# Seven products for all six chunks of a first matmul, in two passes, with two input sums on GpSimd and a group's output assembled in the next group

## The chip, the cores and the metric

The kernel runs on one core of a Trainium2 chip. The metric is the device time of one execution in microseconds (us); less is better. Five engines work side by side, each with its own queue of instructions in program order: TensorE (PE in the profile, with its weight loads as PEld), VectorE (DVE), ScalarE (ACT), GpSimd (POOL) and SyncE (SP), which here only issues DMAs. An instruction waits at the head of its queue until what it needs is there, and everything behind it waits with it.

## The reference, cut to what matters

```python
# x: (8, 4224, 192) float32; weight: (8 heads, 7 taps)
w = softmax(weight, axis=-1)
y[b, s, d] = sum_k w[d // 24, k] * x_pad[b, s + k, d]     # 6 rows of zeros in front of x
xn = (y - mean(y)) / sqrt(var(y) + 1e-6) * g_ln            # over d
out = y + relu(xn @ w_ch1) @ w_ch2                         # 192 -> 768 -> 192
```

Everything is float32. The mean and `g_ln` are folded into the first weight, and 1/sqrt(var) is applied to the result of the second matmul, since relu lets a positive factor through.

## The kernel before, in words

**Tiling.** The rows are cut into 18 groups. Groups 0 to 2 are small and set up the work; groups 3 to 17 have 128 partitions x 16 rows of 192 each, and the change is about those. A group g passes through two matmuls: `up_mixed(g)` (192 to 768, with relu) and `down_fast(g)` (768 to 192). While TensorE works on group g, VectorE finishes the convolution of group g+1 and ScalarE starts that of g+2.

**Seven products.** Both matmuls are done by a scheme that multiplies 2 x 2 blocks with seven products instead of eight, at the price of sums of blocks before and after. A block product has four results c11, c12, c21 and c22; two of the seven products are added into a result that stays in PSUM, others are brought to SBUF (`evict`, a ScalarE copy of the four banks) and added there. `close(c, banks, part)` adds a product to a result already in SBUF: ScalarE copies the banks to a spare tile, and GpSimd issues a DMA that adds that tile to the result (L582). In the last group VectorE adds straight from PSUM instead (L614). In the first matmul the 768 columns are six chunks of 128. Four go through the seven products (2 of each 3, `PAIR`), each product 48 matmul instructions of 256 columns (L521); the two left over are computed plainly (`plain`, 48 matmul instructions of 512 columns each). Products alternate between two sets of four PSUM banks, so a product needs the eviction of the product before the last one. In the second matmul each product is 72 instructions of 256 columns in three steps c (L762), with a ScalarE copy of one bank after each step (L768).

The products of `down_fast` are called d1 to d7 here, in their order: d1 `a[0,0]*b[0]`, d2 `a[1,0]*w2sums[2]`, d3 `a[1,1]*w2sums[3]`, d4 `a[0,1]*b[2]` (no copy, VectorE adds it, L801), d5 `a[1,1]*w2sums[1]`, d6 `a[0,0]*w2sums[0]`, d7 `a[0,1]*b[3]`. d2 needs `lower_sum` (L736); d5, d6 and d7 need the first, second and third triple of the nine `half_sum` instructions (L727) on VectorE. d6 accumulates on the banks of d5 and d7 on those of d6, so each step of d7 needs the copy of the same step of d6.

**Order on the engines around the change.** VectorE, from the start of an `up_mixed(g)`: the output of group g-1 (`finish_fast`: three transposes, an addition, three transposes, L822 and L824), eight tap instructions of the convolution of g+1 (`conv`, L408; each tap is eight instructions, one a head), the last sum of y (L578), 28 taps, `lower_sum`, four taps, then in `down_fast(g)` the transpose of y (L419), ten row statistics (`moments`, L439), `half_sum`, the three additions of d4, six statistics and three sums of y (L574 to L576).

ScalarE: the evictions and closings of the first matmul, with scalings of the output rows of g-1 between them (`scale`, L849, one row each); relus of c11 and c22; then the copies of d1 to d7, between which the first two taps of group g+2 are put (`first_tap` L383 and `second_tap` L394, 16 instructions). The second tap is written to a spare tile `tb` and added to y by two DMAs (L397).

GpSimd issues the adding DMAs: the closings, the taps of `tb`, and `add_to_out` (L856), which adds the scaled output rows to `out` in two halves, rows 0 to 8 and 8 to 16, both within `up_mixed(g)` or just behind it. It also works out 1/sqrt(var) for two groups at a time (`root`, L457 to L470). SP stores y (L477) and loads x.

**Tiles with one buffer.** Each of the pools behind `tb`, `cs`, `ot`, `ys` and `yt` has one buffer. A new tile of such a pool can be written only when all readers of the old one are through, a DMA included. `tb` is in turn the second tap's tile and a room for closings (`parts`). `ot`, the output of a group, is written by the transposes of `finish_fast` and read by the two DMAs of `add_to_out`.

Of the kernel before, what the change touches and what calls it, by code (L numbers as in the profile page):

```python
# [16 lines left out]
def kernel(  # L17
# [34 lines left out]
    P = 128  # L52
# [223 lines left out]
    w1sums = consts.tile([P, 4, CH, PAIR * P], F32, name="w1sums")  # L276
# [236 lines left out]
    def rows_of_tiles(banks, left, right, first=True, last=True):  # L513
# [3 lines left out]
        for c in range(left.shape[2]):  # L517
            for i in range(chunks):
                for q in range(NQ):
                    rows = slice(C * q, C * q + C)  # L520
                    nc.tensor.matmul(  # L521
                        banks[:, q, i * w : i * w + w], right[rows, c, P * i : P * i + P],
                        left[rows, :, c, :], start=(first and c == 0 and i == 0),
                        stop=(last and c == left.shape[2] - 1), skip_group_check=chunks > 1,
                    )
# [22 lines left out]
    def quarters_of_w1():  # L548
        return [
            w1[:, CH * k : CH * k + CH, P * f : P * (f + PAIR)] for k in range(2) for f in (0, FC)  # L550
        ]

    def sums_of_quarters(dst, b11, b12, b21, b22):

        for v, a, b in ((0, b12, b11), (1, b22, 0), (2, b12, b22), (3, b21, 1)):
            a, b = (dst[:, u] if isinstance(u, int) else u for u in (a, b))
            nc.vector.tensor_tensor(dst[:, v], a, b, op=ALU.subtract)
# [10 lines left out]
    def sums_of_y(g):  # L568
# [3 lines left out]
        ysums[g] = s1, s2, s3 = [room[:, v] for v in range(3)]  # L572
        a11, a12, a21, a22 = quarters_of_y(g)
        nc.vector.tensor_tensor(s1, a21, a22, op=ALU.add)  # L574
        nc.vector.tensor_tensor(s2, s1, a11, op=ALU.subtract)
        nc.vector.tensor_tensor(s3, a21, a11, op=ALU.subtract)  # L576
        yield
        nc.vector.tensor_tensor(s2, a12, s2, op=ALU.subtract)  # L578
# [5 lines left out]
    def up_mixed(g, last_sum):  # L584
# [4 lines left out]
        assert groups[g][2] == 2 * HJ and PAIR * W == 512  # L589
# [3 lines left out]
        b11, b12, b21, b22 = quarters_of_w1()  # L593
        s1, s2, s3 = ysums[g]
        (c11, c12), (c21, c22) = [
            [a[:, h, e, 0:PAIR].rearrange("p f q j t -> p f q (j t)") for e in range(2)]
            for h in range(2)
        ]
# [5 lines left out]

        def evict(banks, dst, relu=False, i=slice(0, PAIR)):
            src = banks.rearrange("p q (f w) -> p f q w", w=W)[:, i]
            nc.scalar.activation(dst, src, AF.Relu) if relu else nc.scalar.copy(dst, src)  # L607

        def close(c, banks, part, i=slice(0, PAIR)):


            if last:
                src = banks.rearrange("p q (f w) -> p f q w", w=W)[:, i]
                nc.vector.tensor_tensor(c[:, i], c[:, i], src, op=ALU.add)  # L614
                return
            evict(banks, part, i=i)
            whole = "p f q w -> p (f q w)"
            add_by_dma(c[:, i].rearrange(whole), part.rearrange(whole))

        def plain(f, banks):  # L620
            rows_of_tiles(banks, yt[g][:, 0 : 2 * HJ], w1[:, :, f * P : f * P + P])
            evict_up(g, f, banks)


        chain, other = take_set(), take_set()
        turn[0] += 4
        done = groups[g - 1][2]
        rooms = parts(bpool, "tb"), parts(cpool, "cs")
        first, second = (r[:, 0:PAIR] for r in rooms)
# [8 lines left out]

        rows_of_tiles(chain, a11, b11, True, False)
        evict(chain, c11)  # L640
        rows_of_tiles(other, a12, b21)
        close(c11, other, first)
        rows_of_tiles(chain, s2, w1sums[:, 1], False, False)
        evict(chain, c21)
        act_scales(0, 1)
        taps_of_next(2, 3)
        next(last_sum)
# [8 lines left out]
        rows_of_tiles(other, s3, w1sums[:, 2], True, False)  # L656
        evict(other, c22)
        act_scales(1, 2)
        rows_of_tiles(chain, s1, w1sums[:, 0], False, False)
        close(c22, chain, second)  # L660
        act_scales(2, 3)
        rows_of_tiles(other, a22, w1sums[:, 3], False)
        for i, room in enumerate(rooms):
            close(c21, other, room[:, PAIR : PAIR + 1], slice(i, i + 1))
        act_scales(3, 4)
        rows_of_tiles(chain, s2, b22, False)
        evict(chain, c12, True)
        nc.scalar.activation(c11, c11, AF.Relu)
        act_scales(4, 7)
        taps_of_next(3, 6)  # L670
        taps_of_next(6, K, heads=(0, H // 2))
        plain(PAIR, other)
        nc.scalar.activation(c22, c22, AF.Relu)
        if not last:
            scale(g - 1, 7, 10)
            add_to_out(g - 1, 0, 8)
        lower_sum(g, (PAIR,))
        lower_sum(g, range(PAIR))
        taps_of_next(6, K, heads=(H // 2, H))
        plain(PAIR + FC, chain)  # L680
        if last:

            rest = a[:, 1, 0, 0:PAIR, :, fast[g] :]
            for f in range(PAIR):
                nc.scalar.activation(rest[:, f], rest[:, f], AF.Relu)
        else:
            scale(g - 1, 10, done)
            add_to_out(g - 1, 8, done)
# [54 lines left out]
    def down_fast(g):  # L743
# [254 lines left out]
```

## Time and profile before

| what | us |
| --- | --- |
| median of 3 runs | 969.36 (969.23 to 969.53) |
| span of the profiled execution, first to last instruction | 967.8 |
| TensorE busy in it | 956.1 |
| VectorE busy | 870.7 |
| ScalarE busy | 640.2 |
| one group in the middle (541.76 to 597.73) | 55.97 |
| of it the second matmul, then the first of the next group | 27.33 and 28.64 |

The time of the profiled execution as a whole is not listed apart from its span; the median of the runs is 1.56 us above that span. A line of the timeline gives the start in us from the span's start, the time it took, the engine, the line of the kernel, the operation, output and input, the count of instructions merged into it, and in brackets idle time just before it with what ended it. L12 is line 12 of the kernel.

### The profile page before, as it was taken

How to read it: one execution, taken by the hardware profiler on the slowest of the kernel's cores; microseconds unless marked ns; L12 is line 12 of the kernel's file. 1: busy time of each engine (PE TensorE's matmuls, PEld its weight loads, DVE VectorE, ACT ScalarE, POOL GpSimd, SP SyncE). 2: the span in 40 equal slices, each digit the busy share in tenths (PEclk: the TensorE clock that was granted, in tenths of full speed). 3: DMA queues.
4: the chain of work that ended last, by engine and by line, in shares of the span. 5: the costliest groups of instructions: out<-in, count | busy, mean ns of one | idle time of the engine just before them, and what ended most of it. 6: DMA issues, size and time to landing. Idle time of an engine off the chain costs nothing.

```text
span 967.8 us, 36017 instructions
## 1 busy us (share of the span) xinstructions
PE 956.1 (99%) x16194; PEld 670.3 (69%) x16194; DVE 870.7 (90%) x1489; ACT 640.2 (66%) x1014; POOL 201.1 (21%) x355
## 2 busy tenths in 40 slices
PE   7999999999999999999999999999999999999997
PEld 6886585857668585766758576675857667685767
DVE  7999998898998979898998989899898989989837
ACT  5625677585957758595876858587685858675351
POOL 2005311411133111411114011321104111230400
PEclk9999999999999999999999999999999999999999
DMA  8243887697896869789686978969697886766221
GB/s 204 93 151 109 177 204 224 127 181 211 156 271 126 246 127 192 200 154 271 132 246 125 210 183 150 265 132 253 128 226 170 147 253 136 177 123 110 30 56 68
DMA packets 29960, 163.17 MB, mean 169 GB/s; under 512 B 3567, under 2 KB 9839, under 8 KB 22126
## 3 DMA queue, kind: packets, MB, share of 16 engines
q0 software_dynamic: 22704, 97.53, 53.4%
q1 hardware_dynamic: 6798, 63.34, 17.1%
q8 instruction: 127, 2.08, 0.8%
q14 instruction: 27, 0.22, 0.1%
q10 hardware_dynamic: 304, 0.00, 0.0%
HBM read 38.95 MB, written 50.33 MB: 92 GB/s over the span
## 4 chain that ended last, share of the span: by engine, by line
PE 98%; DMA 1%; DVE 0%; issue 0%; SPq 0%
PE ps L521 49%; PE ps L762 41%; PE ps L707 6%; DMA xg<-in_x_dram 1%; PE ps L320 1%; DMA ga<-in_moe_g_ln_dram 0%; PE ps L344 0%; PE ps L349 0%; DVE y L863 0%; PE ps L332 0%; DVE ot L888 0%; SPq L165 0%; DVE ot L873 0%; DVE y L876 0%
## 5 line engine op out<-in xcount | busy, mean ns | idle before, releaser
L408 DVE SCALAR_TENSOR_TENSOR y<-xg,taps,y 128x384 f32<-128x384 f32 (+3 forms) x734 | 368.1, 580 | 0.7 <-issue 0.5
L521 PE MATMUL ps<-yt,w 32*128 32x256 f32 (+3 forms) x3744 | 287.7, 459 | 0.0
L521 PEld LDWEIGHTS ps<-yt,w 32*128 32x128 f32 x3744 | 188.4, 185 | 90.7 <-issue 80.8
L762 PE MATMUL ps<-room,w2sums 128*32 128x256 f32 (+1 forms) x4320 | 233.8, 375 | 0.0
L762 PEld LDWEIGHTS ps<-room,w2sums 128*32 128x32 f32 x4320 | 140.8, 110 | 87.5
L762 PE MATMUL ps<-room,w 128*32 128x256 f32 (+1 forms) x3240 | 179.8, 375 | 0.0
L727 DVE TENSOR_TENSOR room<-room 128x1024 f32<-128x1024 f32 (+1 forms) x135 | 151.4, 1196 | 9.7 <-ACT part L768 9.7
L762 PEld LDWEIGHTS ps<-room,w 128*32 128x32 f32 x3240 | 104.0, 110 | 74.6 <-ACT ot L849 10.6
L768 ACT COPY cs<-ps 128x256 f32<-128x256 f32 (+1 forms) x180 | 62.9, 366 | 97.8 <-PE ps L762 97.1
L607 ACT COPY room<-ps 128x2048 f32<-128x2048 f32 x45 | 84.0, 1866 | 55.3 <-PE ps L521 53.9
L521 PE MATMUL ps<-ysums,w1sums 32*128 32x256 f32 x2160 | 119.4, 375 | 0.0
L521 PEld LDWEIGHTS ps<-ysums,w1sums 32*128 32x128 f32 x2160 | 110.9, 185 | 5.9 <-DVE room L614 0.3
L824 DVE STREAM_TRANSPOSE ot<-cs 128x512 f32<-128x512 f32 (+1 forms) x90 | 55.9, 672 | 56.8 <-DMA cs<-part 34.5
L511 ACT ACTIVATE room<-ps 128x2048 f32<-128x2048 f32 (+3 forms) x46 | 71.2, 1548 | 33.6 <-PE ps L521 33.6
L849 ACT ACTIVATE ot<-ot,r 128x192 f32<-128x192 f32 x232 | 90.9, 447 | 0.0
L383 ACT ACTIVATE y<-xg,taps 128x384 f32<-128x384 f32 (+3 forms) x141 | 73.3, 589 | 7.5 <-DMA out_dram<-y 6.9
L856 POOL DMA_DIRECT2D out_dram<-ot x40 | 34.2, 1086 | 198.4 <-ACT ot L849 137.1
L439 DVE BATCH_NORM_STATS2 st<-y 128x6 f32<-128x192 f32 x264 | 71.0, 343 | 0.0
L397 POOL DMA_DIRECT2D y<-tb x28 | 24.6, 1037 | 176.2 <-ACT cs L768 172.8
L736 DVE SCALAR_TENSOR_TENSOR room<-room 128x1024 f32<-128x1024 f32 (+1 forms) x45 | 51.5, 1199 | 8.6 <-ACT room L509 7.6
L394 ACT ACTIVATE tb<-xg,taps 128x384 f32<-128x384 f32 x112 | 58.1, 603 | 0.0
L419 DVE STREAM_TRANSPOSE yt<-y 128x3072 f32<-128x3072 f32 (+3 forms) x19 | 56.2, 2957 | 1.9
(104 smaller groups left out, 791.6 us busy)
## 6 DMA issues: line engine op xcount, KB each, us to landing
xg<-in_x_dram SPq DMA_DIRECT2D x15, 2112.0 KB, 15.2
out_dram<-ot POOLq DMA_DIRECT2D x29, 768.0 KB, 8.2
y<-tb POOLq DMA_DIRECT2D x28, 768.0 KB, 9.3
out_dram<-y SPq DMA_DIRECT2D x13, 1536.0 KB, 10.7
room<-parts_tb POOLq DMA_DIRECT2D x14, 1024.0 KB, 7.5
room<-parts_cs POOLq DMA_DIRECT2D x14, 1024.0 KB, 7.1
room<-parts_tb POOLq DMA_DIRECT2D x14, 512.0 KB, 9.3
room<-parts_cs POOLq DMA_DIRECT2D x14, 512.0 KB, 10.8
```

Of the source, the lines that this page charges most:

```text
L383: nc.scalar.mul(y[g][:, 0:n, cs], xg[g][:, 0:n, cs], taps[:, h, 0:1])
L394: nc.scalar.mul(tb[g][:, 0:n, cs], xg[g][:, 1 : 1 + n, cs], taps[:, h, 1:2])
L408: nc.vector.scalar_tensor_tensor(out=y[g][:, 0:n, cs], in0=t[:, k : k + n, cs], scalar=taps[:, h, k : k + 1], in1=y[g][:, 0:n, cs], op0=AL ...
L439: nc.vector.bn_stats(out=sums[g][:, j, :], in_=y[g][:, j, :])
L511: nc.scalar.activation(dst, src, AF.Relu)
L521: nc.tensor.matmul(banks[:, q, i * w : i * w + w], right[rows, c, P * i : P * i + P], left[rows, :, c, :], start=(first and c == 0 and i = ...
L607: nc.scalar.activation(dst, src, AF.Relu) if relu else nc.scalar.copy(dst, src)
L707: nc.tensor.matmul(bank[C * q : C * q + C, 0:w], w2[:, f, C * c : C * c + C], left, start=(f == 0), stop=(f == NF - 1),)
L727: nc.vector.tensor_tensor(a[:, *dst, f], a[:, *left, f], a[:, *right, f], op=op)
L762: nc.tensor.matmul(dst[C * q : C * q + C, 0:w], right[:, f, C * c : C * c + C], left[:, f, q], start=(first and f == 0), stop=(f == FC - 1 ...
L768: nc.scalar.copy(to[:, c], dst[:, 0:w].rearrange("p (j t) -> p j t", t=t))
L849: nc.scalar.mul(ots[g][:, j, :], ots[g][:, j, :], rstd[g][:, j : j + 1])
```

## The change

All six chunks of the first matmul go through the seven products, in two passes: pass one with the third chunk of each half (products of 24 instructions, evictions half as wide), pass two with the other two (products of 48, as before). The two plain products are gone. The sums of the weight are wider, and one is put in place of a block of the weight. In pass two the closing of c21 is done by VectorE from PSUM.

Two of the four sums of y are computed by GpSimd (`sums_of_y(g + 1, nc.gpsimd)`), behind the transpose; the other two follow on VectorE at the end of `down_fast`.

`finish_fast` of group g-1 moves from the end of `down_fast(g-1)` to between the two passes of `up_mixed(g)` (`ahead`), and its first half is added by VectorE from a part in the hidden tile instead of by a DMA. Of the scalings and additions to `out`, the rows from 3 on and both DMAs move into `down_fast` (`ending`), as does the relu of c22 of pass two. All 16 row statistics stand before `half_sum`, all eight instructions of the last tap behind `lower_sum`, and the taps of g+2 are spread otherwise: 4 behind d3, 6 behind d4, 6 behind d5.

```diff
-    w1sums = consts.tile([P, 4, CH, PAIR * P], F32, name="w1sums")
+    w1sums = consts.tile([P, 3, CH, FC * P], F32, name="w1sums")
...
-    def sums_of_y(g):
+    def sums_of_y(g, engine):
...
-        nc.vector.tensor_tensor(s1, a21, a22, op=ALU.add)
-        nc.vector.tensor_tensor(s2, s1, a11, op=ALU.subtract)
-        nc.vector.tensor_tensor(s3, a21, a11, op=ALU.subtract)
+        ysums[g] = a21, s2, s3, s4
+        engine.tensor_tensor(s3, a21, a11, op=ALU.subtract)
+        engine.tensor_tensor(s2, s3, a22, op=ALU.add)
         yield
-        nc.vector.tensor_tensor(s2, a12, s2, op=ALU.subtract)
+        nc.vector.tensor_tensor(s4, a12, s2, op=ALU.subtract)
+        nc.vector.tensor_tensor(a21, a21, a22, op=ALU.add)
         yield
...
+            def close(self, c, banks, part=None):
+                if part is None or last:
+                    nc.vector.tensor_tensor(c, c, self.seen(banks), op=ALU.add)
+                    return
+                self.evict(banks, part)
+                whole = "p f q w -> p (f q w)"
+                add_by_dma(c.rearrange(whole), part.rearrange(whole))
...
+        X, Y = take_set(), take_set()
+        one, two = Pass(PAIR, FC, X, Y), Pass(0, PAIR, Y, X)
+        room1 = parts(bpool, "tb")
+        p = one
+        p.product(X, a11, p.b11, True, False)
+        p.evict(X, p.c11)
+        p.product(Y, a12, p.b21)
+        p.close(p.c11, Y, room1[:, 0:1])
+        p.product(X, s2, p.t[0], False, False)
+        p.evict(X, p.c21)
+        p.product(Y, s3, p.t[1], True, False)
+        p.evict(Y, p.c22)
+        p.product(X, s1, p.b12, False, False)
+        p.close(p.c22, X, room1[:, 1:2])
+        p.product(Y, a22, p.t[2], False)
+        p.close(p.c21, Y, room1[:, 2:3])
+        p.product(X, s4, p.b22, False)
+        p.evict(X, p.c12, True)
+        next(ahead)
+        p = two
+        room2 = parts(cpool, "cs")
+        room3 = parts(bpool, "tb")
+        p.product(Y, a11, p.b11, True, False)
+        p.evict(Y, p.c11)
         act_scales(0, 1)
+        p.product(X, a12, p.b21)
+        p.close(p.c11, X, room2[:, 0:PAIR])
+        act_scales(1, 2)
...
+        p.product(Y, s2, p.t[0], False, False)
+        p.evict(Y, p.c21)
         act_scales(2, 3)
+        p.product(X, s3, p.t[1], True, False)
+        p.evict(X, p.c22)
+        one.relu(one.c11)
+        one.relu(one.c22)
+        p.product(Y, s1, p.b12, False, False)
+        taps_of_next(2, 5)
+        taps_of_next(5, 6, heads=(0, H // 2))
+        p.close(p.c22, Y, room3[:, 0:PAIR])
+        p.product(X, a22, p.t[2], False)
+        taps_of_next(5, 6, heads=(H // 2, H))
+        p.relu(p.c11)
+        p.close(p.c21, X)
+        p.product(Y, s4, p.b22, False)
+        p.evict(Y, p.c12, True)
         lower_sum(g, (PAIR,))
         lower_sum(g, range(PAIR))
-        taps_of_next(6, K, heads=(H // 2, H))
-        plain(PAIR + FC, chain)
...
+        taps_of_next(6, K)
+        def ending(step):
+            if step == 0:
+                two.relu(two.c22)
+            if last:
+                return
+            cuts = [min(j, done) for j in (3, 6, 10, 13, J)]
+            if step < len(cuts) - 1:
+                scale(g - 1, cuts[step], cuts[step + 1])
+            if step == 1:
+                add_to_out(g - 1, 0, 8)
+            if step == 3:
+                add_to_out(g - 1, 8, done)
+        return ending
...
-        taps_behind = [1, 4, 4, 7, 0, 0]
         product(0, a[:, 0, 0], b[0], c11, True)
-        some_taps(taps_behind[0])
+        ending(0)
         product(1, a[:, 1, 0], w2sums[:, 2], c22, True)
-        some_taps(taps_behind[1])
-        product(1, a[:, 1, 1], w2sums[:, 3], parts[0], False)
-        some_taps(taps_behind[2])
+        ending(1)
+        product(1, a[:, 1, 1], w2sums[:, 3], c21, False)
+        some_taps(4)
         product(1, a[:, 0, 1], b[2], None, True)
-        some_taps(taps_behind[3])
+        some_taps(6)
         if g + 1 < NG:
             transpose(g + 1)
-            moments(g + 1, 0, EARLY)
+            sums = sums_of_y(g + 1, nc.gpsimd)
+            next(sums)
+            moments(g + 1)
         half_sum(g, (1, 1), (1, 1), (1, 0), ALU.add)
         half_sum(g, (0, 0), (1, 1), (0, 0), ALU.add)
         half_sum(g, (0, 1), (0, 1), (1, 1), ALU.subtract)
...
-        product(0, a[:, 1, 1], w2sums[:, 1], c21, False)
-        if g + 1 == NG:
-            finish_fast(g, 0, flat, cs, parts)
-        else:
-            close_by_dma(c21, parts[0])
-        some_taps(taps_behind[4])
-        product(0, a[:, 0, 0], w2sums[:, 0], parts[1], False)
-        some_taps(taps_behind[5])
-        product(0, a[:, 0, 1], b[3], c12, False)
-        some_taps(len(todo))
+        product(0, a[:, 1, 1], w2sums[:, 1], parts[0], False)
+        some_taps(6)
+        ending(2)
+        product(0, a[:, 0, 0], w2sums[:, 0], parts[1], False)
+        some_taps(len(todo))
+        ending(3)
+        product(0, a[:, 0, 1], b[3], c12, False)
+        if g + 1 < NG:
+            next(sums)
...
+    def ahead(g):
+        if results is not None:
+            for half in range(2):
+                finish_fast(g - 1, half, *results)
+        yield
```

## The prediction

> **What bounds the kernel now.** First the page's busy shares and the chain that ended last:
>
> ```profile
> span 967.8 us, 36017 instructions
> ...
> PE 956.1 (99%) x16194; PEld 670.3 (69%) x16194; DVE 870.7 (90%) x1489; ACT 640.2 (66%) x1014; POOL 201.1 (21%) x355
> ...
> PE 98%; DMA 1%; DVE 0%; issue 0%; SPq 0%
> ```
>
> TensorE never waits; its granted clock is full throughout. A shorter TensorE program pays only as long as VectorE, at 90%, and the hand-written queues keep up. So next, VectorE's timeline over one group, from `lower_sum`:
>
> ```profile
> 541.61 3.49 DVE L736 SCALAR_TENSOR_TENSOR room<-room 128x1024 f32<-128x1024 f32 x3
> 545.02 2.20 DVE L408 SCALAR_TENSOR_TENSOR y<-xg,taps,y 128x384 f32<-128x384 f32 x4
> 547.32 3.38 DVE L419 STREAM_TRANSPOSE yt<-y 128x3072 f32<-128x3072 f32 x1
> 550.63 2.66 DVE L439 BATCH_NORM_STATS2 st<-y 128x6 f32<-128x192 f32 x10
> 553.20 10.29 DVE L727 TENSOR_TENSOR room<-room 128x1024 f32<-128x1024 f32 x9
> ...
> 573.00 1.90 DVE L824 STREAM_TRANSPOSE ot<-cs 128x512 f32<-128x512 f32 x3 [4.23 <-DMA cs<-part]
> 574.82 0.92 DVE L822 TENSOR_TENSOR cs<-cs,room 128x768 f32<-128x768 f32 x1
> 575.84 1.90 DVE L824 STREAM_TRANSPOSE ot<-cs 128x512 f32<-128x512 f32 x3
> 577.66 4.28 DVE L408 SCALAR_TENSOR_TENSOR y<-xg,taps,y 128x384 f32<-128x384 f32 x8
> ```
>
> VectorE idles once, 4.23 us. The first three `half_sum` are done at 553.20 + 2 x 1.135 (its spacing) + 1.22 = 556.7; d5, which needs them, starts at 557.32. That margin, 0.6 us, is what the change moves first. Then TensorE's timeline:
>
> ```profile
> 569.09 5.46 PE L521 MATMUL ps<-yt,w 32*128 32x256 f32 x96
> 574.38 7.95 PE L521 MATMUL ps<-ysums,w1sums 32*128 32x256 f32 x144
> 582.14 2.77 PE L521 MATMUL ps<-yt,w1sums 32*128 32x256 f32 x48
> 584.74 2.77 PE L521 MATMUL ps<-ysums,w 32*128 32x256 f32 x48
> 587.33 10.48 PE L521 MATMUL ps<-yt,w 32*128 32x512 f32 x96
> ```
>
> The 336 instructions of 256 columns take 587.33 - 569.09 = 18.24 us, 54.3 ns each; a product of 48 is 2.60, one of 24 is 1.30. The plain part takes 10.40 (next line at 597.73). A product of `down_fast` is 27.34 / 7 = 3.91. Last, the DMA list (KB, median us from issue to landing) and two pieces of ScalarE's timeline:
>
> ```profile
> out_dram<-ot POOLq DMA_DIRECT2D x29, 768.0 KB, 8.2
> y<-tb POOLq DMA_DIRECT2D x28, 768.0 KB, 9.3
> ```
>
> ```profile
> 555.49 4.15 ACT L394 ACTIVATE tb<-xg,taps 128x384 f32<-128x384 f32 x8
> 559.54 0.35 ACT L768 COPY cs<-ps 128x256 f32<-128x256 f32 x1
> ```
>
> Today taps on ScalarE make a copy late, and nothing waits for it.
>
> **TensorE's work.** Removed: 10.40 + 18.24. Added: 7 x (24 + 48) = 504 instructions of the shape of L521, 27.34. Saved 1.30 a group, 19.5 over 15 groups. Alone, the group falls from 55.97 to 54.68.
>
> **First wait: d5 on `half_sum`.** The last product but one of pass two now ends 2.60 before d1, and VectorE closes c21 from it. From that end VectorE has: start 0.3 (L614 in the last group began 910.54, its product ended about 910.2), close 2.25 (that row is 2.29), `lower_sum` 3.41, eight taps 4.4 (4.2 and the gap before the transpose), transpose 3.31, 16 statistics 4.14 (2.57 + 1.57 by spacing), three `half_sum` 3.49, handover 0.1 (seen after L614): 21.4. TensorE in that time: 2.60 + 4 x 3.91 + two thirds of d5's first step 0.87 = 19.1. **d5 waits 2.3 us** in each group 3 to 16. VectorE reaches the close in time (below), so its earlier slack doesn't help. The relu of c22 (`ending(0)`) may hold d3 up to 0.9: c22's DMA leaves 2.0 before d1 (its copy stands behind two relus of 1.0) and lands 5.3 after d1's start (7.1 and 7.5 in the 1024 KB rows), relu 1.9, three scales 1.0, then d2's copy 0.4, against 7.8. That lies inside the 2.3.
>
> **Second wait: d7 on ScalarE.** Behind d5's last copy stand six taps of g+2 and three scalings, before d6's copies, the first of which d7 needs. Counted from d5's end: 0.14 to start and 0.27 for the copy, taps 6 x 0.52 = 3.11, scales 3 x 0.34 = 1.03, copy 0.37, handover 0.05: 4.97 against 3.91. **d7 waits 1.06 us** in groups 3 to 15.
>
> The loop of TensorE is now 54.68 + 2.3 + 1.06 = 58.0, already above 55.97.
>
> **Third wait: `tb`** (times from d5's end again). Today the pair of DMAs that adds the second tap goes out at 503.95, 9.2 before `up_mixed` starts at 513.12. Now the tap ends 3.5 after d5 and GpSimd issues the pair from 3.65 on, 5.2 before; the second lands 10.95 after the first's issue (median of the groups from 4 on; 9.6 to 12.4), at 14.6. Pass one's first closing writes into `tb`'s buffer: copy 1.02, handover 0.1, 15.7. `up_mixed` starts at 3.91 + 1.06 + 3.91 = 8.88, and its fourth product, which needs those banks, at 12.78. **2.9 us**; ScalarE's later evictions queue behind, two of 0.91 against products of 1.30, so they catch up. Without this wait evictions of 1.02 in products of 1.30 cost 0 to 0.1 each; I take 0. Loop of TensorE: 58.0 + 2.9 = 61.0.
>
> **Fourth: `ot`.** The second `add_to_out` leaves after d6's copies and three scalings: 4.55 + 0.8 + 1.13 + 0.1 = 6.6 after d5. `finish_fast` writes `ot`'s only buffer, so VectorE stops before its first transpose until the landing. From there: `finish_fast` 4.66 (573.00 to 577.66), 32 taps 16.94, then as above 2.25 + 3.41 + 4.4 + 3.31 + 4.14 + 3.49: 42.6, handover 0.1, rest of d5 3.03. With a landing of 8.2 that loop is 60.5, with 9.9 (median of the second halves today, which travel beside y's store and x's load) 62.2, with 7.0 (first halves) 59.3. I take 8.2: those two now go out earlier, but the `tb` pair is just ahead. So 61.0 holds, with `tb` and `ot` nearly equal. `root` and pass one's closings queue on GpSimd behind this issue; `root` takes 7.9 and is through at d5 + 15.5, when the first closing arrives: nothing.
>
> **What else moves.** VectorE is busy 51.4 a group; two sums less (1.9), close 2.25 and one addition 0.92 more: 52.7, no bound by itself. ScalarE (40.2 a group) evicts 25 pieces of 1024 elements a partition for the 22 of today, 0.95 each: 43.1, hidden but in the two places above. GpSimd issues the same number of closings: three of 512 KB for two, none for `cs<-part` (384 KB). Pass one's third closing leaves about 11.3 after `up_mixed`'s start and lands 10.9 later at most, 22.2; pass two's room in the same buffer is written at 2.9 + 9.1 + 13.0 = 25.0: covered by 2.8, and past that each us would hold ScalarE and the next product. The first `add_to_out` leaves about 10 after d1's start and lands by 18, before `ot` is rewritten. `finish_fast` passes into the gap before the taps; its reads of the parts end about 11 after the start of `up_mixed`, before pass two's c21 (20) overwrites them. `lower_sum` is done 6 after c21's product, d2 starts at 6.5: it holds, by 0.5.
>
> **The sums on GpSimd.** No row of that size. Its additions of 128x16 and 128x32 take 221 and 252 ns: 1.9 ns an element, 1.7 us for 768. Ends: 0.95 (VectorE's) and 6.0 (252 x 24). I take 1.7: both are done 3.4 after the transpose, under 4.14 of statistics; even 12 us lie ahead of their reader, at the end of `half_sum`. Contention, by rows:
>
> ```profile
> 511.72 0.95 POOL L459 TENSOR_TENSOR d<-d 128x32 f32<-128x32 f32 x1
> 512.77 0.21 POOL L451 TENSOR_SCALAR v<-v 128x32 f32<-128x32 f32 x1
> 513.35 0.25 POOL L462 TENSOR_TENSOR v<-v,d 128x32 f32<-128x32 f32 x1
> ```
>
> Beside VectorE's sum of y (511.54 to 512.57) GpSimd took 0.95 instead of 0.25, and VectorE 1.03 instead of 0.95. So VectorE loses about 0.1 to GpSimd: 0. The Trainium skill, "SBUF — State Buffer", Who interferes with whom, says that a VectorE instruction with two SBUF inputs and a GpSimd instruction that reads SBUF exclude each other for the whole instruction, whoever starts first. By that page a sum that outlasts the statistics would hold the first `half_sum` up to a whole sum. By the rows the group stays 61.0; by the page, if that happened, an estimated 62.7.
>
> **Ends.** Start of `up_mixed(3)` 121.3 as before (the wider weight sums, four x 0.4, and one more sum end before its third product). Its first closing waits for `tb` till 126.94 as ScalarE does today: d5 of group 3 ends at 121.3 + 24.74 + 2.9 + 21.4 + 3.03 = 173.4. Group 4 another 61 (no scalings behind the taps: 1.06 less, 1.06 more at `tb`). Then 12 loops to group 16: 234.4 + 732 = 966.4. Group 16 has no taps: last `up_mixed` at 974.2; it takes 27.34 and about 1.3 of waits for closings by VectorE, 28.7 (28.99 before). Behind it 967.8 - 933.9 = 33.9 as before. Span 1036.8; the median stands 1.56 above the profiled span: **1038.4**.
>
> **Rivals.** (1) No DMA binds, 58.0 a group: for it, y's store and x's load, which share the engines with the `tb` pair today, may be through by then; against it, the pair would have to land within 8.0, and 9.6 is the fastest seen (1.6 of the wait left, 59.6 a group, 1021). 13 loops of 3.0 less: 1000. (2) DMAs land late or the lock bites: `ot` 11.1 (seen in five groups) gives 63.4, 12 x 2.4 more: 1067. Down stages already keep the DMA engines 97% busy. (3) The other side: d5 doesn't wait, because VectorE's stretch from c21's close to the third `half_sum` is at most 19.1 instead of 21.4, ScalarE's six taps don't stand before d6's copies, and TensorE alone sets 54.68: 967.8 - 19.5, so 950. The first decides: up to a stretch of 19.1 the 1.30 is kept, 20.4 gives it all back. No row is 1.0 shorter than taken. That the products don't shrink has nothing for it: same instruction shape.
>
> **How the numbers follow.** Likeliest (`tb` and `ot` bind) 0.56, own range 1018 to 1055; (1) 0.22; (2) 0.17; (3) 0.05. The range leaves out (3) and the half of (2) above 1068, together 0.14, and reaches 10 below (1), for a first or second wait that is smaller by 0.8: 990 to 1068. About 0.2% (2 us) is what measurement tells from no change: slower 0.95, same 0.01, faster 0.04.
>
> **What would show it.** TensorE idle at d5 behind L727's line for 2 to 3 us, at d7 behind ScalarE for 1, in pass one behind ScalarE, itself waiting for the DMA from `tb`; VectorE idle before its first output transpose behind the DMA from `ot`; about 61 us from group to group, TensorE near 90%. Wrong if d5 starts 15.6 after d1 without a pause, if `tb` lands before 12 after d5, or if GpSimd's sums stretch the statistics.

## The result: 12.2% slower, and the profile after

| | us |
| --- | --- |
| kernel before, median of 4 runs | 969.44 (969.23 to 970.13) |
| changed kernel, median of 4 runs | 1088.08 (1086.92 to 1089.79) |
| ratio, with its 95% interval | 1.1221 (1.1205 to 1.1237) |
| predicted | 1038.4, range 990 to 1068 |
| span of the profiled execution after | 1085.9 |
| one group, mean of 13 (starts of d1, 153.65 to 993.56) | 64.61, predicted 61.0 |

The direction came as predicted. The loop that sets the time, through the one buffer of `ot`, was in the prediction as well, but as the second longest, at 60.5 us a group; it proved the longest. The time is 50 us above the forecast and 20 above the range. The page of the changed kernel, its span, busy shares, one group of instructions and two DMA rows (KB each, median us from issue to landing):

```profile
span 1085.9 us, 38303 instructions
...
PE 977.6 (90%) x17274; PEld 740.3 (68%) x17274; DVE 893.3 (82%) x1491; ACT 685.6 (63%) x1083; POOL 230.5 (21%) x383
...
L857 DVE STREAM_TRANSPOSE ot<-cs 128x512 f32<-128x512 f32 (+1 forms) x90 | 55.9, 672 | 152.5 <-DMA out_dram<-ot 104.1
...
out_dram<-ot POOLq DMA_DIRECT2D x29, 768.0 KB, 12.3
y<-tb POOLq DMA_DIRECT2D x28, 768.0 KB, 9.1
```

TensorE was 99% busy and is 90% busy now. VectorE's greatest idle time is the 152.5 us ahead of the output transposes, nearly all of it in 13 waits of 9.2 to 12.2, 11.6 on average. The landing of `out_dram<-ot`, 8.2 before, is 12.3; that is a median over both halves. The second halves alone, which matter here, land 11.3 to 12.5 after their issue, 11.9 at the median, where those of before took 8.2 to 11.5. The page's chain of work that ended last breaks off after 8% of the span and can't be read here, so the reading goes by the waits (who waited, for whom: us in total, times, longest):

```profile
DVE ot L857 <- DMA out_dram<-ot: 104.1, 9, 12.2
DVE ot L857 <- ACT room L616: 46.9, 4, 11.9
PE ps L521 <- ACT parts_tb L616: 42.2, 28, 4.5
```

Nine of the 13 waits are put down to the DMA, four to a ScalarE copy that ended at about the same moment; but in all 13 VectorE goes on 0.12 to 0.19 after the landing, so it is the DMA in these four too. VectorE's timeline over a group, to be held against the one in the prediction:

```profile
580.46 1.90 DVE L857 STREAM_TRANSPOSE ot<-cs 128x512 f32<-128x512 f32 x3 [11.58 <-DMA out_dram<-ot]
...
585.12 16.98 DVE L408 SCALAR_TENSOR_TENSOR y<-xg,taps,y 128x384 f32<-128x384 f32 x32
602.02 2.28 DVE L622 TENSOR_TENSOR room<-room,ps 128x2048 f32<-128x2048 f32 x1
...
615.28 4.21 DVE L439 BATCH_NORM_STATS2 st<-y 128x6 f32<-128x192 f32 x16
619.41 10.74 DVE L764 TENSOR_TENSOR room<-room 128x1024 f32<-128x1024 f32 x9
...
645.33 1.90 DVE L857 STREAM_TRANSPOSE ot<-cs 128x512 f32<-128x512 f32 x3 [11.58 <-ACT room L616]
```

From the first transpose to the end of the third `half_sum` VectorE runs without a gap. It comes to c21's close (602.02) some 3 us after TensorE is done with the product, so d1 waits, and again d5. TensorE in the same group:

```profile
566.57 4.09 PE L797 MATMUL ps<-room,w 128*32 128x256 f32 x72 [0.94 <-ACT room L803]
...
577.57 1.58 PE L521 MATMUL ps<-ysums,w1sums 32*128 32x256 f32 x24 [2.60 <-ACT parts_tb L616]
...
599.28 2.87 PE L521 MATMUL ps<-ysums,w 32*128 32x256 f32 x48 [0.46 <-ACT parts_tb L616]
604.40 5.63 PE L797 MATMUL ps<-room,w 128*32 128x256 f32 x72 [2.25 <-ACT room L616]
...
623.39 7.11 PE L797 MATMUL ps<-room,w2sums 128*32 128x256 f32 x128 [0.49 <-DVE room L764]
```

In this order: d7 (566.57), pass one's fourth product, pass two's last, d1 and d5. The profile puts d1's wait down to ScalarE's copy of c12, which ended at 604.10; but d1 starts 0.10 after VectorE's close of c21 has left its PSUM banks (602.02 + 2.28), and in d5's kernel below it starts without waiting for that copy. And GpSimd's issues at that place, with the two sums of y of the next group:

```profile
565.53 1.77 POOL L397 DMA_DIRECT2D y<-tb  x2 [10.67 <-ACT tb L394]
568.40 0.87 POOL L889 DMA_DIRECT2D out_dram<-ot  x1 [1.09 <-ACT ot L882]
...
615.91 2.16 POOL L575 TENSOR_TENSOR ysums<-yt 128x768 f32<-128x768 f32 x1
618.15 1.83 POOL L576 TENSOR_TENSOR ysums<-ysums,yt 128x768 f32<-128x768 f32 x1
630.40 1.77 POOL L397 DMA_DIRECT2D y<-tb  x2 [10.41 <-ACT tb L394]
633.27 0.87 POOL L889 DMA_DIRECT2D out_dram<-ot  x1 [1.09 <-ACT ot L882]
```

The second addition to `out` goes out at 568.40, and VectorE goes on at 580.46: 12.1 us. The pair from `tb` and the addition behind it land one after another, at 571.68, 576.41 and 580.33. The loop of the prediction, with the durations of the next group: d5 ends about 626.4, the DMA is issued at 633.27 (6.9 later), VectorE goes on at 645.33 (12.1); 580.46 to 623.39 is the stretch to d5 going on (42.9), and the rest of d5 takes 3.0. Together 64.9, and the group takes 64.87.

### The profile page after: what moved, and what is told of

It reads as the page before. It is cut to its first block, busy times and chain, and to the rows that moved or that the text cites. A ratio compares the mean times of both kernels' runs of the same rounds, so it can differ in the third digit from the quotient of the medians.

```text
span 1085.9 us, 38303 instructions
## 1 busy us (share of the span) xinstructions
PE 977.6 (90%) x17274; PEld 740.3 (68%) x17274; DVE 893.3 (82%) x1491; ACT 685.6 (63%) x1083; POOL 230.5 (21%) x383
## 5 line engine op out<-in xcount | busy, mean ns | idle before, releaser
L521 PE MATMUL ps<-yt,w 32*128 32x256 f32 (+2 forms) x4104 | 240.5, 381 | 0.0
L521 PEld LDWEIGHTS ps<-yt,w 32*128 32x128 f32 x4104 | 208.5, 188 | 25.8 <-issue 7.0
L797 PEld LDWEIGHTS ps<-room,w 128*32 128x32 f32 x3240 | 112.9, 110 | 100.5 <-issue 17.9
L857 DVE STREAM_TRANSPOSE ot<-cs 128x512 f32<-128x512 f32 (+1 forms) x90 | 55.9, 672 | 152.5 <-DMA out_dram<-ot 104.1
L616 ACT COPY room<-ps 128x1024 f32<-128x1024 f32 (+1 forms) x90 | 129.6, 1440 | 75.9 <-PE ps L521 75.9
L521 PE MATMUL ps<-ysums,w1sums 32*128 32x256 f32 x2160 | 135.0, 395 | 35.7 <-ACT parts_tb L616 35.7
L616 ACT COPY parts_tb<-ps 128x1024 f32<-128x1024 f32 (+1 forms) x56 | 68.5, 1223 | 57.4 <-DMA y<-tb 44.8
L583 POOL DMA_DIRECT2D room<-parts_tb x56 | 48.3, 862 | 249.9 <-ACT parts_tb L616 177.2
L629 ACT ACTIVATE room<-room 128x1024 f32<-128x1024 f32 (+1 forms) x60 | 87.5, 1486 | 1.4 <-DMA room<-parts_tb 1.4
L521 PE MATMUL ps<-ysums,w 32*128 32x256 f32 x1080 | 65.8, 382 | 6.5 <-ACT parts_tb L616 6.5
L803 ACT COPY room<-ps 128x256 f32<-128x256 f32 (+1 forms) x90 | 30.2, 364 | 60.6 <-PE ps L797 57.4
## 6 DMA issues: line engine op xcount, KB each, us to landing
xg<-in_x_dram SPq DMA_DIRECT2D x15, 2112.0 KB, 14.8
out_dram<-ot POOLq DMA_DIRECT2D x29, 768.0 KB, 12.3
```

The lines of the kernel that those rows point to most:

```text
L521: nc.tensor.matmul(banks[:, q, i * w : i * w + w], right[rows, c, P * i : P * i + P], left[rows, :, c, :], start=(first and c == 0 and i = ...
L583: nc.gpsimd.dma_start(out=dst, in_=src, accum_op=ALU.add)
L629: nc.scalar.activation(c, c, AF.Relu)
L797: nc.tensor.matmul(dst[C * q : C * q + C, 0:w], right[:, f, C * c : C * c + C], left[:, f, q], start=(first and f == 0), stop=(f == FC - 1 ...
L803: nc.scalar.copy(to[:, c], dst[:, 0:w].rearrange("p (j t) -> p j t", t=t))
L857: nc.vector.transpose(ot[:, 0:n, C * c : C * c + C], flat[:, c].rearrange("p (j t) -> p j t", t=C))
```

## The experiments

Three theories stood at the start. **A**: the one buffer of `ot` sets the loop, through the landing of the second addition to `out`. **B**: the waits that TensorE shows add up, so that each of them can be taken off by itself. **C**: the sums on GpSimd slow VectorE. The kernel before was run on the same chip each time; there its median was 972.8 to 973.7, so the ratios are what is to be compared. The runs x1 to x9 are two executions each, and the intervals of x2, x3 and x5 cover the changed kernel's ratio.

| run | us, median | ratio to before (95%) |
| --- | --- | --- |
| changed kernel | 1088.08 | 1.122 (1.1205 to 1.1237) |
| x5, sums on VectorE | 1090.18 | 1.120 (1.116 to 1.124) |
| x3, closings not in `tb` | 1096.05 | 1.126 (1.118 to 1.133) |
| x2, `half_sum` ahead of the statistics | 1096.36 | 1.126 (1.112 to 1.140) |
| x1, output ahead of the taps | 1108.93 | 1.139 (1.136 to 1.142) |
| x6, one DMA of the `tb` pair left out | 1041.61 | 1.070 (1.068 to 1.072) |
| x8 = x1 + x5 | 1079.51 | 1.109 (1.106 to 1.112) |
| x9 = x8 + x3 | 996.54 | 1.024 (1.021 to 1.026) |
| d3, everything moved | 981.34 | 1.0087 (1.0068 to 1.0106) |
| d4, x loaded behind the `tb` pair | 975.32 | 1.0019 (1.0008 to 1.0030) |
| d5, closings exchanged | 970.17 | 0.9961 (0.9947 to 0.9975) |
| b1, kernel before with sums on GpSimd | 973.18 | 1.0005 (0.9997 to 1.0014) |

**x6: less ahead in the queue.** Only the first of the two DMAs from `tb` is issued, so half the rows lack their second tap; the run is a measurement and no version of the kernel:

```diff
-            for j1, j2 in ((0, n // 2), (n // 2, n)):
+            for j1, j2 in ((0, n // 2),):
```

> Leaves out the second of the two DMAs that add the second tap to y (rows 8 to 16 get no second tap); the rest is the changed kernel. Theory A with the bytes ahead: the second addition to out lands 12 us after its issue because two transfers of 768 KB are ahead of it; with one, it lands after about 8, VectorE's idle time before the output transposes falls from 11.6 to about 7.5, and the group from 64.6 to 60.6, 1036 us (a little more where TensorE, now paced by c21's closing less, keeps its 0.9 at d7). Rival: the landing is long because GpSimd is busy with root, or because adding into DRAM is slow: still 12, 64.6, 1088.

Its DMA row and the same VectorE line:

```profile
out_dram<-ot POOLq DMA_DIRECT2D x29, 768.0 KB, 9.8
```

```profile
557.43 1.90 DVE L857 STREAM_TRANSPOSE ot<-cs 128x512 f32<-128x512 f32 x3 [8.61 <-DMA out_dram<-ot]
```

One transfer of 768 KB less ahead of it, and the addition to `out` lands 2.5 us earlier by the row's median (3.0 for the second halves alone, 8.9 for 11.9), VectorE waits 3.0 less, and the group takes 61.2 (mean of 13) where it took 64.6. That is A: the loop follows the landing. The wait of pass one for `tb` is gone here too, so the run by itself could also be B's; x3 takes that apart.

**x3: pass one's closings elsewhere.** The three spare pieces come from chunks of the hidden tile that pass two writes later:

```diff
-        room1 = parts(bpool, "tb")
+        room1 = [a[:, h, e, f : f + 1].rearrange("p f q j t -> p f q (j t)")
+                 for h, e, f in ((0, 1, 0), (0, 1, 1), (1, 1, 0))]
```

> The three closings of pass one go through free chunks of the hidden tile (c12 and c22, not yet written) instead of tb's buffer, so TensorE's wait of 2.6 to 2.7 us in pass one is gone. Theory A: VectorE sits waiting for ot at that time, so the group stays 64.6 and the time 1085 to 1089; TensorE's wait moves to the start of d1, which needs c21's closing. Theory B: 13 times 2.7 less, about 1053. Theory C: no change, 1088.

TensorE's 2.6 us in pass one are gone, and the time is not less. VectorE's wait is as it was, and TensorE makes up the difference at d1, which here too begins 0.1 after VectorE's close of c21 (609.09 + 2.28):

```profile
587.53 1.90 DVE L860 STREAM_TRANSPOSE ot<-cs 128x512 f32<-128x512 f32 x3 [11.56 <-DMA out_dram<-ot]
```

```profile
611.47 6.16 PE L800 MATMUL ps<-room,w 128*32 128x256 f32 x72 [5.02 <-issue]
```

A, against B: a wait of an engine that isn't the loop only moves. The group takes 65.2, 0.6 more than A has it. In most groups the sums on GpSimd start later here and run into `half_sum`, whose first three take 4.0 on average instead of 3.5: here C costs something.

**x5: the two sums back on VectorE**, at the end of `down_fast`.

```diff
-            sums = sums_of_y(g + 1, nc.gpsimd)
-            next(sums)
+            sums = sums_of_y(g + 1, nc.vector)
...
         if g + 1 < NG:
+            next(sums)
             next(sums)
```

> The two sums of y that GpSimd computes are back on VectorE, behind half_sum, 1.9 us of work. Theory A: VectorE then waits 1.9 less for ot, the loop is the same: 64.6 a group less at most 0.4 for half_sum's stretch beside GpSimd's sum in some groups, 1082 to 1089 us. Theory C: GpSimd's sums and their hold on the shared port are what costs: well under 1080.

VectorE's wait for `ot` in this run:

```profile
585.35 1.90 DVE L857 STREAM_TRANSPOSE ot<-cs 128x512 f32<-128x512 f32 x3 [9.42 <-DMA out_dram<-ot]
```

No difference in the time (the intervals overlap). VectorE's 1.9 us more fall into its wait for `ot`, which shrinks from 11.58 to 9.42. C falls for the changed kernel, though a trace of contention is there: the nine `half_sum` take 10.29 here in every group. In the changed kernel they take 10.3 in 13 groups of 14, and 10.74 in the one shown above, where the second sum on GpSimd ran 0.6 into them.

**b1: that part alone, on the kernel before.** a21 + a22 and that minus a11 on GpSimd, at the place where VectorE had them.

```diff
-        nc.vector.tensor_tensor(s1, a21, a22, op=ALU.add)
-        nc.vector.tensor_tensor(s2, s1, a11, op=ALU.subtract)
+        nc.gpsimd.tensor_tensor(s1, a21, a22, op=ALU.add)
+        nc.gpsimd.tensor_tensor(s2, s1, a11, op=ALU.subtract)
```

> The kernel before, with one part of the change alone: two of the sums of y (a21 plus a22, and that minus a11) on GpSimd, where VectorE had them at 0.95 us each. The theory that the sums on GpSimd are no cost by themselves: they run beside VectorE's 4.2 us of waiting for the closing of c21, VectorE has about 1.9 a group less, and TensorE's product after half_sum is untouched, so 968 to 970 against 969.4. The rival, that a GpSimd operation of this size slows VectorE's two-input operations or is locked out by them: the sum is stretched past the transposes and the taps, TensorE's product with s2 waits for it, 3 to 10 us a group by the 11.0 us that one sum took in the run with the output ahead of the taps, so 1005 or more.

The same time as the kernel before on that chip. VectorE's third sum beside them took 2.03 us for 0.95, and it costs nothing, since VectorE then waits for a DMA anyway.

**x2: `half_sum` first.** The first triple stands ahead of the 16 statistics, to take d5's wait away:

```diff
-            moments(g + 1)
         half_sum(g, (1, 1), (1, 1), (1, 0), ALU.add)
+            moments(g + 1)
```

> The first three half_sum instructions stand before the 16 row statistics instead of behind them. Theory A: the statistics (4.1 us) leave the loop; GpSimd's two sums of 1.84 now run beside half_sum and can hold it up by up to one of them: 60.5 to 62.4 a group, 1034 to 1059 us. Theory B: the wait at d5 as the trace shows it, 0.5 to 1.5 us a group, goes: about 1075. Theory C: half_sum meets GpSimd's sums head on and the group gets longer: over 1088.

A missed, for three reasons that the trace shows. d6 needs the second triple, which is still behind the statistics, so TensorE waits 2.16 there instead. The two sums on GpSimd now start before `half_sum`, whose first three take 6.01 instead of 3.49. And these first wait 1.48 for TensorE, whose d3 reads the block that they write:

```profile
563.10 6.01 DVE L764 TENSOR_TENSOR room<-room 128x1024 f32<-128x1024 f32 x3 [1.48 <-PE ps L797]
```

So d5 came hardly earlier, and the group took 65.0. The time is the one that C named, but two executions as far apart as 1090.83 and 1101.90 can't tell it from the changed kernel's. The run bears on the landing too. Here the addition to `out` goes out 5.6 after the pair (576.17 and 581.74) instead of 2.9, with all the bytes as before, and lands 9.5 after its issue instead of 11.9: 15.1 after the pair's issue, against 14.8 in the changed kernel. So most of the landing is the wait for the pair ahead; the addition itself is through 3.9 behind it (576.41 to 580.33 in the changed kernel).

**x1: the output ahead of the taps.** All scalings of group g-1 and both additions to `out` go ahead of the taps of g+2, so that `ot` is free early:

```diff
-            cuts = [min(j, done) for j in (3, 6, 10, 13, J)]
+            cuts = [min(j, done) for j in (3, 6, 11, J)]
-            if step == 3:
+            if step == 2:
                 add_to_out(g - 1, 8, done)
...
         product(1, a[:, 1, 1], w2sums[:, 3], c21, False)
+        ending(2)
         some_taps(4)
...
         some_taps(6)
-        ending(2)
...
         some_taps(len(todo))
-        ending(3)
```

> All scalings of the output rows and both additions to out now stand on ScalarE and GpSimd before the six last taps and the tb pair; nothing else differs from the changed kernel. Theory A (the buffer of ot): the group of 64.6 us is the loop from d5's end over the second addition to out, its landing 12 us later, the output's transposes, 32 taps, c21, lower_sum, eight taps, transpose, statistics and half_sum back to d5. The landing then comes before VectorE gets there, the idle 11.6 us before the first output transpose shrink to under 2, and TensorE's own waits are left: 54.7 + 2.3 at d5 + 0.5 before the last product of pass two + 3 to 4 at tb, 60 to 61 a group, about 1035 us in all. Theory B (the waits of TensorE add up, each for what it shows): only the wait of 0.94 at d7 goes, about 1076. Theory C (GpSimd's sums slow VectorE): no change, 1088.

The wait for `ot` is gone, as A wanted, and the kernel is slower still, above what all three theories had. GpSimd and TensorE in the changed order:

```profile
567.49 0.87 POOL L888 DMA_DIRECT2D out_dram<-ot  x1 [4.21 <-ACT ot L881]
568.06 11.02 POOL L575 TENSOR_TENSOR ysums<-yt 128x768 f32<-128x768 f32 x1
579.16 1.83 POOL L576 TENSOR_TENSOR ysums<-ysums,yt 128x768 f32<-128x768 f32 x1
580.93 1.78 POOL L397 DMA_DIRECT2D y<-tb  x2
```

```profile
591.51 2.94 PE L521 MATMUL ps<-ysums,w1sums 32*128 32x256 f32 x24 [5.46 <-ACT parts_tb L616]
```

The first sum now stands behind the second addition to `out` in GpSimd's queue and starts 0.96 after the nine `half_sum` did (567.10). It ends at 579.08, 0.7 after they and the small additions behind them are through (577.31 + 1.07): 11.0 us for an operation of 1.84. Behind it in the queue stands the `tb` pair, which goes out 7.3 after d5's end (573.67) in place of 4.0; behind that wait pass one's first closing, and TensorE. The `half_sum` were not stretched (10.29). So the sums were innocent only at the place that they have in the changed kernel.

**x8: the edits of x1 and x5 together**, the output early and no sum on GpSimd.

> The early additions to out of the run before last, now with the two sums of y on VectorE behind half_sum, so that no GpSimd sum stands between the second addition to out and the tb pair. Theory A, completed by what the run with early additions showed (GpSimd's first sum, issued when half_sum has begun, was held 11 us and the tb pair behind it): the pair goes out 3.6 after d5 again, TensorE waits 3 to 4 at tb and 1.5 to 2.3 at d5 and loses up to 2 to a lower granted clock behind the longer pause: 60 to 62.5 a group, 1028 to 1060 us. Rival (GpSimd's hold was not the cause of 5.5 at tb in that run): about 1108 as there.

Better than either, but 20 us above the expectation, 63.6 a group. VectorE waits no more for `ot`, it waits for TensorE (6.80 ahead of c21's close). TensorE waits for `tb`, in the place of the prediction's third wait and longer, and its 24 instructions after that take 2.94 instead of 1.58:

```profile
595.63 2.29 DVE L622 TENSOR_TENSOR room<-room,ps 128x2048 f32<-128x2048 f32 x1 [6.80 <-PE ps L521]
```

```profile
572.89 2.94 PE L521 MATMUL ps<-ysums,w1sums 32*128 32x256 f32 x24 [3.73 <-ACT parts_tb L616]
```

With the loop through `ot` cut, the loop through `tb` is the longest.

**x9: the edits of x8 and x3 together.**

> As the run above, and pass one's closings go through the hidden tile instead of tb. Theory A: now that ot no longer holds VectorE, TensorE's wait at tb is a cost in full and goes: 54.7 + 2.3 at d5 + 0.5 before the last product of pass two, 57 to 58.5 a group (VectorE's taps may still wait for the tb pair), 995 to 1010 us. Rival (waits merely move to the next place, as when the closings alone were moved): as the run above.

As expected: 57.4 a group. The edit that was worth nothing in x3 is worth 83 us here. What is left is mostly ScalarE, whose copies of d2 stand behind three scalings and a relu, which itself waits 2.19 for a closing's DMA, and make d3 wait:

```profile
623.03 4.09 PE L800 MATMUL ps<-room,w2sums 128*32 128x256 f32 x72 [1.89 <-ACT cs L806]
```

**d3: everything moved.** The edit of x3 again, and besides: all scalings and both additions to `out` ahead of the taps of g+2; the sums on VectorE behind the statistics; the relu of c22 of pass one later; scalings only behind the copies of d2 and d3; taps spread 1, 9 and 6; `half_sum` behind three statistics and ahead of 13; c21's first half added by a DMA as in the kernel before. The core of it:

```diff
+            cuts = [min(j, done) for j in (3, 3, 10, J)]
...
-            moments(g + 1)
+            moments(g + 1, 0, 3)
         half_sum(g, (1, 1), (1, 1), (1, 0), ALU.add)
...
+            add_by_dma(*(v.rearrange("p c j t -> p c (j t)") for v in (c21, parts[0])))
...
+            moments(g + 1, 3)
```

> Everything the theory names, moved: closings of pass one in the hidden tile; scalings and additions to out before the taps (1 tap behind d1, 9 behind d4, 6 behind d5); half_sum before 13 of the 16 statistics; sums of y on VectorE behind the statistics; c21's first half added by DMA again; one relu of pass one behind the copy that the last product of pass two waits for. VectorE's work is 53.7 a group and TensorE's 54.7. Theory A: 54.7 to 56 a group, between 950 and 975 us: level with the kernel before or up to 2% faster. If a wait is left that the theory doesn't name, over 985.

981, a little above what was expected, 56.6 a group. In nearly all groups TensorE waits only at d1, 1.3 to 1.6, since VectorE's taps wait 2.5 to 2.8 for the second of the `tb` pair. The profile names no releaser, but the times tell: the pair goes out at 573.21, its second half lands at 587.05, and the taps begin at 587.22. That line, and the run's DMA row for the output:

```profile
587.22 17.02 DVE L408 SCALAR_TENSOR_TENSOR y<-xg,taps,y 128x384 f32<-128x384 f32 x32 [2.74 <-issue]
```

```profile
out_dram<-ot POOLq DMA_DIRECT2D x29, 768.0 KB, 13.5
```

**d4: x loaded behind the pair**, on GpSimd's queue for the group after next, no longer on SP's (the clearing of its padding moves with it):

```diff
         some_taps(6)
+        if g + 3 < NG:
+            load_x(g + 3, nc.gpsimd)
```

> The kernel of the run before (everything moved: closings of pass one into hidden-tile space, the output's ending before the taps, sums of y on VectorE behind the statistics), with one transfer moved: the load of x, about 2.1 MB a group, no longer goes out early on SP's queue but on GpSimd's queue behind the pair y<-tb, for the group after next. In the run before, VectorE still waited 2.7 us a group for the second of that pair, which landed some 14 us after its issue, with the load of x, the store of y, the adds to out and a closing under way at once. If those bytes made it late, the pair lands 10 to 11 after its issue (as it did in the changed kernel), the taps' wait of 2.7 and the 1.5 that TensorE then waits at d1 go, and the group takes 54.7 to 55.5 in place of 56.9: 13 x 1.4 to 2.2 = 18 to 29 off the 981.3, so 952 to 963 (that chip's kernel before was 973.7). If the pair is late for what lies ahead of it in its own queue, nothing moves: 979 to 984. If the load of x then comes late for the taps of the group after next, they wait at another place and the time is above 985.

The same DMA row in this run:

```profile
out_dram<-ot POOLq DMA_DIRECT2D x29, 768.0 KB, 8.3
```

The taps' wait is gone in most groups and 0.3 to 1.2 in five, and `out_dram<-ot` lands in 8.3 instead of 13.5, with x's load moved. In d3 that load (558.24) had landed at 571.95, before the pair went out; so it can have made the pair late only through the transfers ahead of the pair, the last of which landed at 579.60. The time, 975, is above the 952 to 963 expected: the best groups take 55.3, but the mean is 56.1. ScalarE's copy into pass two's c22 waits for the third closing of pass one, which still lies in that chunk.

```profile
819.42 1.87 ACT L617 COPY room<-ps 128x2048 f32<-128x2048 f32 x1 [2.50 <-DMA room<-room]
```

**d5: the first closing in that chunk**, the other two where c12 comes last:

```diff
-            for h, e, f in ((0, 1, 0), (0, 1, 1), (1, 1, 0))
+            for h, e, f in ((1, 1, 0), (0, 1, 0), (0, 1, 1))
```

> The kernel of the run before (everything moved, x behind the tb pair), with one thing exchanged: which of pass one's three closings waits in which free chunk of the hidden tile. There the third closing (c21's) lay in the first chunk of pass two's c22, and ScalarE's copy into that c22 waited up to 2.5 us for that transfer to leave (14.7 over 12 groups); TensorE then stood 0.4 to 1.6 at pass two's sixth product, and the closing behind it came late for the third product of the second half (1.2). Now the first closing lies there and the other two where c12 comes last. If TensorE's own work is all that is then left, every group takes 55.3, what the best groups of the run before took, in place of 56.08: 14 x 0.8 = 11 less, 964 on that chip, 0.991 of the kernel before; I expect 964 to 969. This also tells the size of the saving: the prediction had 54.68 against 55.97 for TensorE's own work; 55.3 means that half of it goes into the switches between the shorter products. If another transfer takes the place (c12's chunks still busy when c12 is copied, or VectorE's taps late), the time stays at 972 to 978.

970.17, 0.4% faster than the kernel before, and the only version here that is. I had expected 964 to 969. About half the groups reach what TensorE's work takes, the others wait up to 1.5 at d1 for the relu of pass two's c11, or, in one group, 0.9 at d3 for that of c22, each relu behind a closing's DMA. A group without waits (stretch, us, busy us of TensorE, its weight loads, VectorE, ScalarE and GpSimd with their instructions, granted clock, DMA share, GB/s):

```profile
711.67:766.89 55.22, 55.22 (x1009) 41.26 (x1009) 53.64 (x85) 43.02 (x67) 18.43 (x31) 1.00 0.87 200
```

## Why the prediction was wrong

**The step that failed** is the fourth wait: "With a landing of 8.2 that loop is 60.5 … I take 8.2: those two now go out earlier, but the `tb` pair is just ahead. So 61.0 holds". The landing is 11.9, and 12.1 until VectorE goes on. The loop by the prediction's own terms is then 6.6 + 12.1 + 42.7 + 3.0 = 64.4, and 64.6 was measured. So the order of the two loops failed with the size: the prediction let TensorE's own loop, through `tb`, set 61.0, and that one had slack. 13 loops of 3.6 more are 47 us; the first d1 came 2.1 later than the sum of the ends has it. 1036.8 + 47 + 2.1 = 1085.9, the measured span. That the landing is the term, and the pair ahead in the queue its cause, x6 and x2 show; x's load has no part in it in the changed kernel, since it is issued at 612.83, lands at 626.33, and so is through before the pair goes out at 630.40.

The row that would have given it was in the trace of before, in GpSimd's timeline:

```profile
559.92 1.75 POOL L397 DMA_DIRECT2D y<-tb  x2 [12.93 <-ACT cs L768]
562.12 1.28 POOL L582 DMA_DIRECT2D cs<-part  x1 [0.45 <-ACT cs L768]
```

That closing, 384 KB, went out 2.2 behind the same pair, and VectorE took it up at 573.00, in the prediction's own fence: 10.9 us. The prediction took a median over transfers with nothing or something else ahead, where this one had the same two ahead. By their landings in that trace the second of the pair was through at 570.84 and the closing at 572.88: 2.04 for 384 KB, so an estimated 4.1 for 768. That makes 10.9 + 4.1 = 15.0 after the pair's issue, and 12.1 after that of the addition, which goes out 2.9 later. 11.9 was measured.

**The loop through `ot` was rival (2) in kind**, with 11.1 and 1067. Its landing was still a microsecond short, and it got 0.17: "DMAs land late" stood there as something that may happen, not as what the pair ahead brings about in every group.

**First wait, d5 2.3.** It is 0.5 to 1.5 in the changed kernel. Its terms held (21.4 from c21's close at 602.02 to d5 at 623.39, 21.1 by the prediction's terms), but VectorE comes late to c21, and in most groups d1 waits 0.8 to 3.3 for it first, 2.25 in the one shown. One lateness shows in two places of the trace.

**Second wait, d7 1.06**: 0.94. **Third, `tb` 2.9**: 2.60 in the group shown, 1.9 to 4.5 over the groups. **Issue of the addition, 6.6 after d5**: 6.8 to 6.9. **VectorE's stretch 42.7**: 42.9. These held. Not foreseen is 0.46 at pass two's last product, where ScalarE's copy for c22 stands behind two relus.

**TensorE's work, 1.30 a group saved.** d5 is the test, and the term was too good. Without any wait a group takes 55.22, not 54.68: the 504 instructions of the first matmul need 27.8 instead of 27.34 (504 at the prediction's 54.3 ns are 27.36), and the second matmul 27.45. "Evictions of 1.02 in products of 1.30 cost 0 to 0.1 each; I take 0" was too good: in d5 TensorE's weight loads wait 44 times for evictions, about three times a group, 0.3 at the longest. So the change as d5 orders it can give 55.98 - 55.22 = 0.76 a group, some 11 us, and d5 has 2.6 of them by the medians, 3.8 by the ratio. With every wait gone that is an estimated 958, not the third rival's 950.

**The sums on GpSimd.** 1.84 to 2.16 against 1.7 taken: the estimate held. "VectorE loses about 0.1 to GpSimd: 0" holds only for the changed kernel's order. The prediction weighed against it the Trainium skill, "SBUF — State Buffer", Who interferes with whom, by which a two-input VectorE instruction and a GpSimd instruction that reads SBUF exclude each other. x1 and x2 bear it out, on one side each: 11.0 for 1.84 on GpSimd, 6.01 for 3.49 on VectorE. In the changed kernel it cost 0.45 in the `half_sum` of one group of 14, the one shown; in x3 about 0.5 a group on average.

## What to carry to other kernels

Take a DMA's landing from a row that has the same bytes ahead of it in its queue, not from the median of its kind; here 8 became 12. What other queues move at that time counts too: x's load was worth 5 us of landing (d3 against d4). Where a tile has one buffer, write down the whole loop through its last reader before anything is moved towards that reader, and look for the next longest loop beside it, for cutting one only shows the next: the same edit was worth nothing in x3 and 83 us in x9. What is moved past an instruction in an in-order queue (GpSimd's sum behind a DMA issue) takes all that stands behind it along.

## What was not expected of the hardware

**TensorE's granted clock can fall after a pause of 2 us or more.** d1 in the changed kernel takes 5.63 after a pause of 2.25 where it takes 4.09 otherwise, and the profile has the granted clock at 0.50 from 604.16 to 607.58, one of seven such stretches there, six of 3.41 us and one of 6.83; in x3 6.16 after 5.02; in x1 the 24 instructions after 5.46 take 2.94 instead of 1.58. The mean granted clock was 1.000 before, 0.987 in the changed kernel, 0.955 in x1, 0.966 in x8 and 1.000 in x9. It isn't the length of the pause alone: after 2.60 (at 577.57 above) nothing fell. The Trainium skill, "TensorE: Matmul & The Clock Gate", The HAM clock gate, describes a gate that halves the clock until some 3.4 us of activity, by a free-running window; the stretches of 3.41 us fit, and pauses shorter than that window were enough here. The loss was hidden in the changed kernel, where TensorE waits at d1 or d5 anyway; in x1 and x8 VectorE waits for TensorE (7.20 and 6.80 ahead of c21's close), so there it most likely stood in the loop.

**A short GpSimd operation can be kept out for ten microseconds** by VectorE instructions that follow each other without a gap (x1: 11.02 for 1.84, and 9.2 to 11.4 in 13 of its 14 groups).

What stays open: why waits of 0.4 to 1.5 come up in some groups of d5 and not in others, and how much of x's load would have to go elsewhere to be rid of them. A second buffer for `ot`, the most direct test of that loop, was not tried.
